# One core, attention and gated feed-forward: P times V of every fourth key tile as three f16 products

## The chip, the core and the metric

The kernel runs on one core of one Trainium2 chip. The metric is the device time of one execution in microseconds (us). Engine names are those of the profile: PE is TensorE's matmuls and PEld its weight loads, DVE is VectorE, ACT is ScalarE, POOL is GpSimd, SP is the queue that issues most DMAs.

## The reference

A block of 2048 rows of width 512, cut to what matters:

```python
h = layernorm(x) * (1 + ca) + sa            # sa, ca, ga, ... = six parts of silu(c) @ w_mod
q = (h @ wq) as 32 heads of 16;  k = h @ wk;  v = h @ wv      # one key and value head for all
p = softmax(q @ k.T * 16 ** -0.5)           # 32 heads x 2048 queries x 2048 keys
x = x + ga * ((p @ v) @ wo)
h = layernorm(x) * (1 + cb) + sb
x = x + gb * (((h @ w_gate) * (h @ w_up)) @ w_down)
```

All inputs are f32. The kernel keeps close to f32 by writing an operand as the sum of two f16 halves and taking three f16 products (high by high, low by high, high by low).

## The kernel before, in words

**Units and turns.** Queries go in 8 blocks of 256 rows, heads in 4 groups of 8. A unit is one group on one block; there are 32 units (0 to 31) of 16 key tiles of 128 keys. `attend(u, kt)` handles key tiles kt and kt+1 of unit u in two turns. In each turn PE computes four score tiles (`qk_exp`, line 648: keys on the rows, 2 heads' parts by 512 columns) and ACT takes the exponential of each (line 661), giving a 128x512 f32 tile of P. At the end of a turn `end_turn` (line 1229) runs `pv` (line 665) for the key tile before: P times V, four f32 matmuls 32 columns wide, one on each quarter of PE's columns, added up in a bank of PSUM over the 16 key tiles. Columns 16 to 31 of V's tile are ones, so the row sums come with it. After the last key tile `pv_out` (line 673) copies the bank out with a factor, `evs`, on ACT (line 676), one turn later.

**The order of a turn** is written out in strings (lines 58 to 60). The one for most of the kernel is

```python
MANY = "x1 e0 x1 m0 x1 e0 x1 e0 x1 m0 x1 m0 x1 m0 x1 e0"
```

An `e` is a score tile with its exponential. An `m` is a matmul for the row maxima of a unit ahead, which DVE reduces (line 605); the maxima enter the scores as two extra rows of the query operand. An `x` is half a step of side work: projections, output projection, gate, up and down (`Group`, line 491; its matmuls are at line 511). Scores and maxima use one half of PE's 128 rows and side work the other, so they run in pairs; the halves are swapped every turn. Since a side bank is then added to from other rows, the first side matmul of a turn waits for the last exponential of the turn before (`sync`, line 527), which follows the last side matmul of that turn.

**Side work around the change.** Each block of 256 rows passes the output projection, the second layer norm, 14 gate and up groups and two down groups. A gate and up group ends with ACT (line 847), DVE (849) and two Pool instructions (850, 851), which write the f16 halves of the gated product to the tile `glu`, double buffered by block. Late weights are staged in slots of the tile `kwb` and split by Pool during units 0 to 8 (`SLOTS`, line 35).

**Order on the engines.** Each engine works in the order in which the program lists its instructions. PSUM has 8 banks, handed out in turn.

The first 66 us hold the layer norm, keys, values, and the row maxima of unit 0.

Of the kernel before, what the change touches and what calls it, by code (L numbers as in the profile page):

```python
# [20 lines left out]
KC = D // 128  # L21
# [13 lines left out]
SLOTS = (0, 1, 2, 3, 6, 7)  # L35
# [6 lines left out]
NBANK = 8  # L42
QPRE = 24
# [20 lines left out]
def adaln_mqa_glu_kernel(ctx: ExitStack, tc: tile.TileContext, x_in, wq_in, wk_in, wv_in, wo_in,  # L64
# [161 lines left out]
    ssqs = [kwb[:, 2 * n * BT:2 * n * BT + 2 * F].bitcast(F32) for n in (KC, 2 * KC)]  # L226
    kng = kwb[:, 2 * NHF * BT:2 * NHF * BT + BT]
# [86 lines left out]
    def v_mm(b):  # L314
        p = ps_hold("pvt", (128, 4, 16))
        for i in range(4):
            nc.tensor.matmul(p[:, i, :], parts[b][:, i * 128:(i + 1) * 128], lane[:, 16:32], start=True, stop=True)

        def out():
            nc.scalar.activation(vst[:, 4 * b:4 * b + 4, 0:16], p, AF.Copy, scale=inv[:, 0:1] if b else 1.0)  # L320
            ps_give(p)
        posts.append(out)
# [48 lines left out]
    kb = consts.tile([128, 8], F32, name="kb")  # L371
    inv = consts.tile([128, 3], F32, name="inv")
# [15 lines left out]
    nc.gpsimd.tensor_scalar(sckb, sck, inv[:, 0:1], 0.0, op0=OP.mult, op1=OP.add)  # L388
    combine(0, selk)
# [9 lines left out]
    evs = consts.tile([128, 1], F32, name="evs")  # L399

    def ev_scales():

        t = work.tile([128, 2], F32, name="evt", bufs=1)
        nc.vector.tensor_reduce(evs, ident.rearrange("p (a r) -> p a r", a=4)[:, :, 0:16], axis=AX.XY, op=OP.add)
        nc.vector.reciprocal(t[:, 0:1], kb[:, 5:6])
        nc.gpsimd.tensor_tensor(t[:, 0:1], t[:, 0:1], evs, op=OP.mult)
        nc.gpsimd.tensor_scalar(t[:, 1:2], evs, -1.0, 1.0, op0=OP.mult, op1=OP.add)
        nc.gpsimd.tensor_tensor(evs, t[:, 0:1], t[:, 1:2], op=OP.add)

# [43 lines left out]
    def last_rows():  # L453
# [21 lines left out]
             15: lambda: h_halves(1, KA), 17: lambda: h_halves(1, KB), 20: ev_scales}  # L475
# [6 lines left out]
    sync = {"due": False, "exp": None, "before": None}  # L482
    pending = []

    def flush():
        for f in pending:
            f()
            sync["due"] = True
        pending.clear()

    class Group:
# [31 lines left out]
        def half(self, r):  # L523

            mm = self.put(r, r + 1)
            if self.rows not in (None, r):
                tc.add_manual_dep(mm.ins, sync["before"], SYNC)
            self.rows, self.turn, sync["due"] = r, now[0], True
            if self.ended():
                ended.append(self)  # L530
# [111 lines left out]
    pvb = {}  # L642
    ptl = {}
    oc = {}
# [3 lines left out]
    def qk_exp(u, kt, p, a, last=False):  # L648
        s = sst[u % 3]
        ptl[u, kt, p, a] = work.tile([128, D], F32, name="P", tag="P", bufs=8)  # L650
        t = ps_sc()
        keys = kst[64 * a:64 * a + 50, kt * 128:(kt + 1) * 128]
        if pending and last:
            for c in range(2):
                if c:
                    flush()
                nc.tensor.matmul(t[:, c * ST:(c + 1) * ST], keys, s[64 * a:64 * a + 50, c, p, :], start=True, stop=True)  # L657
        else:
            nc.tensor.matmul(t.rearrange("k (c n) -> k c n", c=2), keys, s[64 * a:64 * a + 50, :, p, :],  # L659
                             start=True, stop=True)  # L660
        ex = nc.scalar.activation(ptl[u, kt, p, a], t, AF.Exp)  # L661
        if sync["due"]:
            sync.update(due=False, exp=ex.ins.name)

    def pv(u, kt):
        if kt == 0:
            pvb[u] = ps_hold("pv")
        for j in range(4):
            p, a = divmod(j, 2)
            nc.tensor.matmul(pvb[u][32 * j:32 * j + 32, :], vst[:, kt, :], ptl[u, kt, p, a],  # L670
                             start=(kt == 0), stop=(kt == KT - 1))

    def pv_out(u):
        sb, ch = divmod(u, NC)
        ev = work.tile([128, BT], F32, name="ev", tag="ev", bufs=3)
        nc.scalar.activation(ev, pvb[u], AF.Copy, scale=evs)
# [115 lines left out]
    def ln2_work(sb):  # L792
        st = {}

        def tr(i):
            def f():
                if not h2s:
                    h2T = big.tile([128, 2, 2, KC, ST], F16, name="h2T", tag="wq")
                    glus.append(big.tile([128, 2, 2, FT, ST], F16, name="glu", tag="big"))
                    h2s.update({s: h2T[:, s % 2] for s in range(NS)})  # L800
# [31 lines left out]
    def ffn_work(sb):  # L832

        def glu():
            return glus[0][:, sb % 2]
# [57 lines left out]
    def late_weights():  # L893
# [37 lines left out]
        def stage(n):  # L931
            if "d" in W:
                t = work.tile([128, D], F32, name="wsl", tag="xl", bufs=3)
            else:
                t = hfs[:, SLOTS[taken[0] % len(SLOTS)], :]
# [237 lines left out]
    side = deque(wlist)  # L1173
# [44 lines left out]
    def attend(u, kt):  # L1218
# [7 lines left out]
        orders = [[(w[0], int(w[1:] or 0)) for w in s.split()] for s in (style if style is NO_SIDE else (style, style))]  # L1226
        count = {}

        def end_turn(kt):
# [5 lines left out]
            ends.clear()  # L1235
            v = u * KT + kt - 1
# [77 lines left out]
    pv(u, KT - 1)  # L1314
    pv_out(u)
# [61 lines left out]
```

## Time and profile before

| | us |
|---|---|
| median of 3 runs (lowest to highest) | 1665.17 (1664.72 to 1667.52) |
| span of the profiled execution, first to last instruction | 1663.8 |
| that execution's own time around the span | not given apart; the median is 1.4 longer than the span |
| PE busy | 1643.3 |
| DVE busy | 1402.3 |
| ACT busy | 1234.8 |
| POOL busy | 523.5 |

A row of the timeline gives the start from the span's beginning, the length, the engine, the line, the operation, what it writes and reads, and how many like instructions were merged. A row of the groups gives the busy time of all and the mean of one in ns. A row of the table by stretches gives, for each engine, busy us and the number of instructions. An f32 matmul appears as two matmul records, each passing over its columns twice.

### The profile page before, as it was taken

To read this page: it belongs to the slowest core of one execution; us is meant where nothing else is said; L and a number is where in the kernel's file an instruction comes from. 1 tells how busy PE (TensorE), PEld (TensorE's weight loads), DVE (VectorE), ACT (ScalarE), POOL (GpSimd) and SP (SyncE) were. 2 spreads that over 40 slices of the span, in tenths; PEclk is the share of its full clock that TensorE was granted. 3 is DMA by queue.
4 is the path that set the end of the run, shared out by engine and by line. 5 is a ranking of instruction groups with operands and counts; after the bars stand their busy time and mean duration, and the time that the engine had idled before them with its cause. 6 is when DMAs were issued, how large, how long until landed. Compare 5 with 4: busy or idle time off the path is not lost.

```text
span 1663.8 us, 39821 instructions
## 1 busy us (share of the span) xinstructions
PE 1643.3 (99%) x15677; PEld 747.1 (45%) x15677; DVE 1402.3 (84%) x2434; ACT 1234.8 (74%) x2389; POOL 523.5 (31%) x833
## 2 busy tenths in 40 slices
PE   8899999999999999999999999999999999999999
PEld 4333333355533554335543355434545345454776
DVE  7999999998998999899998999999998999980211
ACT  5688888888777877777877787777878777877300
POOL 4857537864841111301112011300113001210322
PEclk9999999999999999999999999999999999999999
DMA  6313313342210001000000000000000000000100
GB/s 237 108 59 100 95 43 120 96 129 80 77 51 24 18 12 32 19 32 20 20 26 23 25 13 24 26 25 26 20 29 15 26 22 20 26 14 21 33 13 14
DMA packets 66024, 75.39 MB, mean 45 GB/s; under 512 B 17702, under 2 KB 46634, under 8 KB 65836
## 3 DMA queue, kind: packets, MB, share of 16 engines
q1 hardware_dynamic: 63724, 72.26, 13.7%
q8 instruction: 123, 2.02, 0.5%
q10 hardware_dynamic: 2112, 0.59, 0.1%
q14 instruction: 65, 0.53, 0.1%
HBM read 55.51 MB, written 17.04 MB: 44 GB/s over the span
## 4 chain that ended last, share of the span: by engine, by line
PE 93%; ACT 2%; DVE 2%; DMA 1%; issue 1%; POOL 0%; SPq 0%; ACTq 0%; DVEq 0%
PE side L511 41%; PE pv L670 30%; PE mx L601 8%; PE sc L659 8%; PE sc L657 3%; ACT P L661 2%; DVE mpart L605 1%; DMA xbig<-in_A_x_dram 1%; PE mx L805 1%; PE mxt L629 0%; ACT hf L813 0%; PE sc L601 0%; DVE bs L248 0%; DMA kwb<-in_B_w_down_dram 0%; DMA wkv<-in_A_wv_dram 0%
## 5 line engine op out<-in xcount | busy, mean ns | idle before, releaser
L605 DVE TENSOR_REDUCE mpart<-mx 128x1 f32<-128x512 f32 x2016 | 1274.1, 684 | 104.0 <-PE mx L601 95.7
L661 ACT ACTIVATE P<-sc 128x512 f32<-128x512 f32 x2048 | 1094.8, 598 | 274.2 <-PE sc L659 226.9
L601 PE MATMUL mx<-kst,sst 48*128 48x512 f16 x2032 | 631.5, 377 | 3.8 <-ACT P L661 1.7
L659 PE MATMUL sc<-sst,kst 50*128 50x512 f16 x1792 | 597.5, 379 | 0.6 <-ACT P L661 0.3
L670 PE MATMUL pv<-P,vst 128*32 128x512 f32 x4096 | 545.3, 605 | 0.7
L511 PE MATMUL side<-h2T,wg 64*128 64x256 f16 (+1 forms) x2396 | 540.8, 271 | 0.1
L511 PE MATMUL side<-h2T,wu 64*128 64x256 f16 (+1 forms) x2396 | 538.7, 270 | 0.0
L511 PEld LDWEIGHTS <-wg 64*128 64x128 f16 (+1 forms) x2396 | 226.0, 94 | 230.5 <-ACT P L661 194.0
L511 PE MATMUL side<-wd,glu 64*128 64x512 f16 (+1 forms) x1172 | 272.8, 378 | 0.2 <-ACT P L661 0.2
L850 POOL TENSOR_SCALAR glu<-gf 128x256 f16<-128x256 f32 x112 | 45.8, 409 | 671.3 <-DVE gf L849 583.9
L511 PEld LDWEIGHTS <-wu 64*128 64x128 f16 (+1 forms) x2396 | 226.4, 94 | 43.0 <-issue 7.8
L601 PEld LDWEIGHTS <-sst 48*128 48x128 f16 x2064 | 189.9, 94 | 34.2 <-issue 17.4
L659 PEld LDWEIGHTS <-kst 50*128 50x128 f16 x1792 | 162.9, 94 | 63.0 <-issue 50.3
L511 PEld LDWEIGHTS <-glu 64*128 64x128 f16 (+1 forms) x1172 | 98.5, 94 | 192.4 <-ACT P L661 85.9
L670 PEld LDWEIGHTS pv<-P,vst 128*32 128x32 f32 x4096 | 80.7, 108 | 160.9 <-issue 150.1
L849 DVE TENSOR_TENSOR gf<-side,g 128x256 f32<-128x256 f32 x112 | 46.7, 418 | 79.8 <-ACT g L847 77.7
L657 PE MATMUL sc<-sst,kst 50*128 50x256 f16 x512 | 96.9, 268 | 0.1
L511 PE MATMUL side<-h,wq 64*128 64x512 f16 (+1 forms) x372 | 95.0, 376 | 0.4 <-ACT P L661 0.4
L847 ACT ACTIVATE g<-side 128x256 f32<-128x256 f32 x112 | 42.3, 379 | 65.6 <-PE side L511 65.3
L511 PE MATMUL side<-wo,och 64*128 64x512 f16 (+1 forms) x360 | 86.3, 377 | 0.0
L851 POOL TENSOR_TENSOR glu<-gf,glu 128x256 f16<-128x256 f32 x112 | 75.3, 673 | 9.3
L706 POOL TENSOR_TENSOR oc<-oc,rr 128x256 f32<-128x256 f32 x31 | 22.7, 731 | 146.6 <-DMA rr<-ri 100.4
(233 smaller groups left out, 865.4 us busy)
## 6 DMA issues: line engine op xcount, KB each, us to landing
pd<-ev SPq DMA_DIRECT2D x32, 256.0 KB
kwb<-in_B_w_gate_dram SPq DMA_DIRECT2D x32, 224.0 KB
kwb<-in_B_w_up_dram SPq DMA_DIRECT2D x32, 224.0 KB
sst<-qd SPq DMA_DIRECT2D x180, 32.0 KB
qd<-q SPq DMA_DIRECT2D x16, 256.0 KB
oc<-pd SPq DMA_DIRECT2D x64, 64.0 KB
rr<-ri SPq DMA_DIRECT2D x64, 64.0 KB
x<-in_A_x_dram SPq DMA_DIRECT2D x14, 256.0 KB
```

The lines of the kernel that those rows point to most:

```text
L511: return nc.tensor.matmul(self.p[:, c * w:(c + 1) * w], left[rows], right[rows], start=start and c == 0, stop=stop and c == len(terms) - 1)
L601: nc.tensor.matmul(m, s[64 * a:64 * a + 48, t // 2, p, t % 2 * 128:(t % 2 + 1) * 128], w[64 * a:64 * a + 48, :], start=(i == 0), stop=(i = ...
L605: nc.vector.tensor_reduce(part, m, axis=AX.X, op=OP.max)
L657: nc.tensor.matmul(t[:, c * ST:(c + 1) * ST], keys, s[64 * a:64 * a + 50, c, p, :], start=True, stop=True)
L659: nc.tensor.matmul(t.rearrange("k (c n) -> k c n", c=2), keys, s[64 * a:64 * a + 50, :, p, :], start=True, stop=True)
L661: ex = nc.scalar.activation(ptl[u, kt, p, a], t, AF.Exp)
L670: nc.tensor.matmul(pvb[u][32 * j:32 * j + 32, :], vst[:, kt, :], ptl[u, kt, p, a], start=(kt == 0), stop=(kt == KT - 1))
L706: eng.tensor_tensor(o, o, st["r"], op=OP.mult)
L847: nc.scalar.activation(g, p[:, 0:ST], AF.Copy, scale=2.0 ** -45)
L849: nc.vector.tensor_tensor(gf, p[:, ST:2 * ST], g, op=OP.mult)
L850: nc.gpsimd.tensor_scalar(glu()[:, 0, f, :], gf, 1.0, 0.0, op0=OP.mult, op1=OP.add)
L851: nc.gpsimd.tensor_tensor(glu()[:, 1, f, :], gf, glu()[:, 0, f, :], op=OP.subtract)
```

## The change

- In units 9 to 31 the key tiles 0, 4, 8 and 12 are split: 92 tiles. Their four P tiles go to one of two sets kept in the tile `glu`, which so far held two blocks of gated products and now holds one. Pool writes each P tile as two f16 halves (`p_halves`, one tile per turn, two instructions). V's halves (`v16`) are made once.
- P times V of a split tile is twelve f16 matmuls with their own weight loads instead of four f32 matmuls. It is put off by four key tiles (`pv_turn`): that of tiles 0, 4 and 8 stands where that of the next split tile stood, at the end of a turn, and that of tile 12 stands behind tile 15's, in the next unit's first turn. The end of the next unit's second turn has no P times V.
- In the turn in which a split tile's last exponential runs, a copy of one number on ACT stands before that exponential. It waits for the turn's last side matmul, and the next turn's first side matmul waits for the copy instead of the exponential.
- 14 times ln 2 is added to the exponent by way of the row maxima, so P is 2^14 times larger: one more DVE instruction per unit. The factor `evs` goes, with its two DVE and three Pool instructions; V is scaled instead by `vsc`, made by a DVE reciprocal and a Pool product in the first 25 us.
- The staged weights use slots 12 and 13 instead of 6 and 7, and the scratch for dynamic DMAs is 256 instead of 4096 bytes.

The diff, cut to its core:

```diff
-SLOTS = (0, 1, 2, 3, 6, 7)
+SLOTS = (0, 1, 2, 3, 12, 13)
+EVERY = 4
+SPLIT_FROM = 5
+P_BIAS = float(14 * np.log(2.0))
...
+    nc.vector.reciprocal(vsc[:, 0:1], kb[:, 5:6])
+    nc.gpsimd.tensor_tensor(vsc[:, 1:2], vsc[:, 0:1], inv[:, 0:1], op=OP.mult)
...
-            sync["due"] = True
+            sync.update(due=True, half=f().ins.name)
...
         nc.vector.tensor_reduce(mms[u], mparts[u], axis=AX.X, op=OP.max)
+        nc.vector.tensor_scalar(mms[u], mms[u], -P_BIAS, None, op0=OP.add)
...
+        if last and sync["early"]:
+            ex = nc.scalar.activation(tok[:, 1:2], tok[:, 0:1], AF.Copy)
+            tc.add_manual_dep(ex.ins, sync["half"], SYNC)
+            sync.update(due=False, exp=ex.ins.name)
         ex = nc.scalar.activation(ptl[u, kt, p, a], t, AF.Exp)
...
+    def p_halves():
+        if todo_p:
+            u, kt, p, a = todo_p.popleft()
+            hi, lo = p_view(split_p[u, kt], 2 * a + p)
+            t = ptl[u, kt, p, a]
+            nc.gpsimd.tensor_scalar(hi, t, 1.0, 0.0, op0=OP.mult, op1=OP.add)
+            nc.gpsimd.tensor_tensor(lo, t, hi, op=OP.subtract)
...
+        for n, (vl, pl) in enumerate(((0, 0), (1, 0), (0, 1))):
+            for j in range(4):
+                p, a = divmod(j, 2)
+                nc.tensor.matmul(pvb[u][32 * j:32 * j + 32, :], v16[:, vl, kt // EVERY, :],
+                                 p_view(split_p[u, kt], 2 * a + p)[pl], start=start and n == 0, stop=stop and n == 2)
+
+    def pv_turn(u, kt):
+        if (u, kt) in split_p:
+            late_p.append((u, kt))
+            if len(late_p) > 1:
+                pv(*late_p.popleft())
+        else:
+            pv(u, kt)
+        if kt == KT - 1:
+            while late_p:
+                pv(*late_p.popleft())
+            ends.append(lambda: pv_out(u))
...
-        nc.scalar.activation(ev, pvb[u], AF.Copy, scale=evs)
+        nc.scalar.activation(ev, pvb[u], AF.Copy)
...
-            return glus[0][:, sb % 2]
+            return glus[0]
...
+        if style is MANY and kt % EVERY == 0 and p_sets and not side_items and (u, kt) > (SPLIT_FROM, 0):
+            split_p[u, kt] = len(split_p) % 2
...
+            p_halves()
             v = u * KT + kt - 1
             if v >= 0:
-                pv(*divmod(v, KT))
-                if v % KT == KT - 1:
-                    ends.append(lambda: pv_out(u - 1))
+                pv_turn(*divmod(v, KT))
...
+            sync["early"] = turn == 1 and (u, kt) in split_p
```

Where instructions stand before and now, at three places. On PE, the end of unit 10's first turn, before (`sc` is a score tile, `side` the side work):

```order
5759 L659 LDWEIGHTS kst
5760 L659 MATMUL sc<-sst_129,kst 128x512
5761 L670 MATMUL pv<-P,vst 32x512 x4
5762 L511 LDWEIGHTS glu
5763 L511 MATMUL side<-wd,glu 128x512
```

and after (`v_341` is `v16`; the rows go on in this way to twelve pairs of load and matmul):

```order
5827 L670 LDWEIGHTS kst
5828 L670 MATMUL sc<-sst_129,kst 128x512
5829 L697 MATMUL pv<-P,vst 32x512 x4
5830 L705 LDWEIGHTS v_341
5831 L705 MATMUL pv<-glu,v_341 32x512
5832 L705 LDWEIGHTS v_341
5833 L705 MATMUL pv<-glu,v_341 32x512
```

Tile 12's twelve matmuls of unit 9 moved here, behind tile 15's four.

On ACT, from the late exponentials of unit 8 to the copy of its bank (`ev`), before:

```order
153 L661 ACTIVATE P<-sc 128x512 x12
154 L847 ACTIVATE g<-side 128x256
155 L661 ACTIVATE P<-sc 128x512 x28
156 L634 ACTIVATE mt_7791<-mxt 16x128
157 L661 ACTIVATE P<-sc 128x512 x16
158 L676 ACTIVATE ev<-pv,evs 128x512
```

and after, where unit 9's first split tile (`glu<-sc`) and the small copy (`tok`) stand:

```order
157 L676 ACTIVATE P<-sc 128x512 x8
158 L676 ACTIVATE glu<-sc 128x512 x2
159 L676 ACTIVATE P<-sc 128x512 x2
160 L676 ACTIVATE glu<-sc 128x512 x2
161 L676 ACTIVATE P<-sc 128x512
162 L673 ACTIVATE tok<-tok 1x1
163 L676 ACTIVATE P<-sc 128x512
164 L723 ACTIVATE ev<-pv 128x512
165 L676 ACTIVATE P<-sc 128x512 x8
```

The copy came in before the turn's last exponential; the bank's copy still stands right behind it, ahead of the next turn's exponentials.

On DVE, in the first 25 us, where the first keys are scaled, before:

```order
32 L386 RECIPROCAL fwd<-inv 128x1
33 L387 TENSOR_SCALAR hsb<-modT_178,fwd 128x8
34 L261 TENSOR_SCALAR xbig<-xbig,st,ry_262 128x512 x2
35 L248 BN_STATS bs<-xbig 128x6 x2
36 L250 BN_AGGR st<-bs 128x2 x2
```

and after:

```order
32 L394 RECIPROCAL fwd<-inv 128x1
33 L395 TENSOR_SCALAR hsb<-modT_178,fwd 128x8
34 L397 RECIPROCAL vsc<-kb 128x1
35 L265 TENSOR_SCALAR xbig<-xbig,st,ry_262 128x512 x2
36 L252 BN_STATS bs<-xbig 128x6 x2
```

A reciprocal of a number that Pool makes (`kb`) came in ahead of the layer norm's work.

More of the change, by code (lines that the diff above doesn't have):

```diff
@@ L398, in adaln_mqa_glu_kernel @@
     ln_norm(1, (None, nc.scalar, None, nc.scalar))
[L399 to L408, printed above, removed]
     qvs = consts.tile([128, 1], F32, name="qvs")
@@ L481, in adaln_mqa_glu_kernel @@
     ended = []
-    sync = {"due": False, "exp": None, "before": None}
+    sync = {"due": False, "exp": None, "before": None, "half": None, "early": False}
     pending = []
@@ L527, in half @@
                 tc.add_manual_dep(mm.ins, sync["before"], SYNC)
-            self.rows, self.turn, sync["due"] = r, now[0], True
+            self.rows, self.turn, sync["due"], sync["half"] = r, now[0], True, mm.ins.name
             if self.ended():
```

60 lines of the change are left out of this document (45 added, 15 removed).

## The prediction

> **What bounds the kernel now.** I read the page first: busy times, then the chain that ended last.
>
> ```profile
> PE 1643.3 (99%) x15677; PEld 747.1 (45%) x15677; DVE 1402.3 (84%) x2434; ACT 1234.8 (74%) x2389; POOL 523.5 (31%) x833
> ...
> PE side L511 41%; PE pv L670 30%; PE mx L601 8%; PE sc L659 8%; PE sc L657 3%; ACT P L661 2%; DVE mpart L605 1%; DMA xbig<-in_A_x_dram 1%; PE mx L805 1%; PE mxt L629 0%; ACT hf L813 0%; PE sc L601 0%; DVE bs L248 0%; DMA kwb<-in_B_w_down_dr
> ```
>
> PE carries the chain, and P times V (L670) is 30% of it. The table by stretches then says how near the others are, early and in the stage that the change is about:
>
> ```profile
> 200.00:300.00 100.00, 99.06 (x815) 31.54 (x809) 96.91 (x173) 81.44 (x158) 60.77 (x88) 1.00 0.26 82
> 1000.00:1300.00 300.00, 299.58 (x3045) 136.91 (x3041) 275.41 (x465) 235.40 (x453) 57.66 (x101) 1.00 0.08 23
> ```
>
> Late, PE is full, DVE at 92%, ACT at 78%, POOL at 19%, clock 1.00. Early DVE is at 97%: there an added DVE instruction costs nearly its length. One per cent off PE's late turns is within reach of the other engines.
>
> Last the timeline of three turn ends, at the boundary from unit 17 to 18:
>
> ```profile
> 900.77 1.06 PE L670 MATMUL pv<-P,vst 128*32 128x512 f32 x8
> 901.77 0.39 PE L511 MATMUL side<-wd,glu 64*128 64x512 f16 x1
> 902.23 2.17 ACT L661 ACTIVATE P<-sc 128x512 f32<-128x512 f32 x4 [0.67 <-PE sc L659]
> 903.29 0.38 PE L511 MATMUL side<-wd,glu 64*128 64x512 f16 x1
> 903.61 0.16 PEld L670 LDWEIGHTS pv<-P,vst 128*32 128x32 f32 x8 [0.43 <-ACT P L661]
> 903.61 1.07 PE L670 MATMUL pv<-P,vst 128*32 128x512 f32 x8
> 904.29 0.68 ACT L676 ACTIVATE ev<-pv,evs 128x512 f32<-128x512 f32 x1
> 904.61 0.39 PE L511 MATMUL side<-wd,glu 64*128 64x512 f16 x1
> 905.12 2.09 ACT L661 ACTIVATE P<-sc 128x512 f32<-128x512 f32 x4
> 906.45 1.06 PE L670 MATMUL pv<-P,vst 128*32 128x512 f32 x8
> 907.44 0.39 PE L511 MATMUL side<-wd,glu 64*128 64x512 f16 x1
> ```
>
> A turn is 2.84 us: 1.84 of pairs (the eighth side matmul starts 1.52 in, so a pair takes 0.217) and 1.00 from P times V's start to the next turn. Call a turn's start T. The four exponentials run from T+0.46 to T+2.63, and the next turn's first matmul, which waits for the last of them, starts 0.21 later. Is that wait or PE the bound? Narrower windows of the timeline answer (the last two rows are of a turn that ACT held up):
>
> ```profile
> 901.23 0.61 PE L670 MATMUL pv<-P,vst 128*32 128x512 f32 x4
> ...
> 903.21 1.18 ACT L661 ACTIVATE P<-sc 128x512 f32<-128x512 f32 x2
> ...
> 903.80 0.60 ACT L661 ACTIVATE P<-sc 128x512 f32<-128x512 f32 x1
> ...
> 1433.59 0.60 ACT L661 ACTIVATE P<-sc 128x512 f32<-128x512 f32 x1
> ...
> 1434.24 0.28 PE L511 MATMUL side<-h2T,wg 64*128 64x256 f16 x1
> ```
>
> The four f32 matmuls run side by side in two rounds, 0.46 apart; the second starts 0.54 before the next turn. That is its 0.43 of columns (two passes of 0.213) and 0.10 for the change of tiling. The sum closes without ACT, and it closes alike in every turn above, so PE's own work sets the turn and the wait is hidden by about 0.15 (0.21 less the 0.05 that the last two rows have from ACT's end to PE). ACT's third and fourth exponentials start at T+1.44 and T+2.03, 0.49 apart when nothing is waited for (four in 2.09, the last 0.60 long).
>
> **P times V in f16, behind a turn (tiles 0, 4, 8: 69 of 92).** No f16 matmul 32 columns wide is in this trace. The nearest rows are f32 ones with half the columns, each two passes of 256, as many steps as one pass of 512:
>
> ```profile
> 19.96 1.08 PE L279 MATMUL part<-kwb,wqs 128*32 128x256 f32 x16
> ...
> L279 PE MATMUL part<-kwb,wqs 128*32 128x256 f32 x64 | 4.1, 384 | 0.0
> ```
>
> Sixteen on four column groups are four rounds: (1.08 - 0.38) / 3 = 0.23 a round, stagger included; a pair of f16 matmuls takes 0.217. I take 0.216 a round, as the stagger is paid once, with 0.235 as the upper bound. Three rounds, 0.02 stagger, 0.02 for the first load and 0.10 for the change of tiling: 0.79 instead of 1.00, a gain of 0.21 (0.15 at the upper bound). 69 x 0.21 = **-14.5**. The lower bound of a round is the columns alone, 0.213, which is nearly my value. The weight loads double in number per round, but the row above has eight loads in the first 0.16 us of an operation whose second round starts 0.46 in: loads run ahead of the matmuls there.
>
> [...]
>
> The copy must be done by then: the last side matmul ends at T+1.90 (903.29 + 0.38), the third exponential frees ACT at about T+1.93, and the copy lasts some 0.17, as other tiny ACT instructions do:
>
> ```profile
> L353 ACT ACTIVATE modT<-misc 128x4 f32<-128x4 f32 x1 | 0.2, 172 | 0.0
> ```
>
> It starts at T+2.01 (0.11 behind the matmul, as exponentials are behind their scores) and frees PE at T+2.24, before P times V's end at T+2.63. Hidden; the last exponential moves from T+2.03 to T+2.16 and ends at T+2.76, still before the next turn's first score.
>
> **Tile 12, behind tile 15's P times V (23 times).** No tiling change more, three rounds: 23 x 0.648 = **+14.9**. So the put-off alone gives back what the shorter products gain.
>
> **The turn that has no P times V (23 times).** The next turn may start at T+2.24, when the copy frees it, not T+2.84: 0.60 gained. But the bank's copy (ev, 0.68) stands right behind the last exponential: it starts at T+2.65 and the next exponential some 0.59 after it, T+3.24, where the turn begun at T+2.24 could have had it at T+2.70. Four exponentials 0.49 apart end at T+5.31, and the turn after starts at T+5.37. Before, two turns took 5.69. The gain is 0.33, not 0.60. In 5 of 23 units a side group's evacuation also stands there, and it falls to about 0.05. 18 x 0.33 + 5 x 0.05 = **-6.2** (bounds: none, and 23 x 0.60 = -13.8).
>
> **Pool's splits.** One P tile costs
>
> ```profile
> L441 POOL TENSOR_TENSOR h<-kwb,h 128x512 f16<-128x512 f32 x12 | 13.9, 1162 | 1.0
> L440 POOL TENSOR_SCALAR h<-kwb 128x512 f16<-128x512 f32 x12 | 7.5, 623 | 0.3
> ```
>
> 1.79 us, 1.95 with two gaps of 0.08: 368 of them are 718 us, 1.95 in every 2.84 us turn on an engine that is 19% busy. It fits, with little room. Tiles 0, 4 and 8 have two turns between the last split's place and its use. Tile 12 has one. What stands ahead of that last split on Pool decides; here a gate and up group ends in that very turn (unit 16, tile 14's P times V at 849.72, tile 15's at 852.56):
>
> ```profile
> 849.72 1.06 PE L670 MATMUL pv<-P,vst 128*32 128x512 f32 x8
> 850.95 0.42 DVE L849 TENSOR_TENSOR gf<-side,g 128x256 f32<-128x256 f32 x1
> 851.45 0.41 POOL L850 TENSOR_SCALAR glu<-gf 128x256 f16<-128x256 f32 x1 [7.70 <-DVE gf L849]
> 851.94 0.67 POOL L851 TENSOR_TENSOR glu<-gf,glu 128x256 f16<-128x256 f32 x1
> 852.56 0.64 PE L670 MATMUL pv<-P,vst 128*32 128x512 f32 x4
> ```
>
> Pool, in order, waits for gf, ends glu at 852.61, the split's high half at 853.3 and its low half at 854.55. PE would start tile 12's products at 853.44 and needs the low half in the third, at 853.9: it stands 0.7. By the order this happens in four units (16, 20, 24, 28), and a lateness of 0.2 in three more (21, 25, 29): **+3.4** (bounds: 0, and 0.8 in each of 23: +18).
>
> Does Pool's load slow DVE? DVE's reductions alone, in the same two stretches:
>
> ```profile
> 200.00:300.00 100.00, 91.16 (x147) 1.00 0.26 82
> 1000.00:1300.00 300.00, 259.69 (x410) 1.00 0.08 23
> ```
>
> 0.620 us each with POOL at 61%, 0.633 with POOL at 19%: no. [...]
>
> **The first 25 us.** The new reciprocal stands ahead of the layer norm's work on DVE and waits for a number that Pool makes (timeline, then two rows by line with their lengths in ns):
>
> ```profile
> 20.88 0.23 DVE L387 TENSOR_SCALAR hsb<-modT,fwd 128x8 f32<-128x8 f32 x1
> 21.02 0.99 DVE L261 TENSOR_SCALAR xbig<-xbig,st,ry 128x512 f32<-128x512 f32 x2
> ...
> 22.15 0.26 POOL L377 TENSOR_SCALAR kb<-kb 128x1 f32<-128x1 f32 x1
> ...
> 23.98 0.74 DVE L304 SCALAR_TENSOR_TENSOR sst<-pk,sck,hi 128x512 f16<-128x512 f32 x1
> ...
> 24.78 0.61 PE L601 MATMUL mx<-kst,sst 48*128 48x512 f16 x4
> ...
> L404 DVE TENSOR_REDUCE evs<-ident x1: 218/218/218, 64.0 to 64.0; 128x1 f32<-128x64 f32 x1
> ...
> L405 DVE RECIPROCAL evt<-kb x1: 155/155/155, 64.1 to 64.1; 128x1 f32<-128x1 f32 x1
> ```
>
> Pool has it at 22.41. DVE, free for L261 at 21.02, now stands until about 22.5 and then does the reciprocal (0.15): L261 and all behind it start 1.6 later. Queued behind are the scaling of keys and queries; sst, done at 24.72, feeds PE's matmul at 24.78, and the transposes stand behind that on PE. No slack: +1.6. The two DVE instructions that go (0.22 and 0.15, at 64 us) give back 0.4: **+1.2**.
>
> **The bias** is a 128x16 DVE instruction per unit, 0.2 us like L387's 0.23. In the DVE-bound stretch
>
> ```profile
> 60.00:300.00 240.00, 1.32 (x6) 1.00 0.28 85
> ```
>
> six units' maxima end (the reduction it follows, L622): at most 6 x 0.2; later DVE's 8% of slack hides it. **+0.8.** The slots, the scratch size and the single block of gated products I put at nothing: the first are staged two steps ahead, and a down group ends on PE before the next block's first gate group starts. If that cover is gone, it shows as Pool waits on DMA or PE.
>
> **The sum.** -14.5 + 14.9 - 6.2 + 3.4 + 1.2 + 0.8 = -0.4. Against the profiled span, 1663.8, that is 1663.4; what lies around the span, 1.4 to the median, stays. Forecast: **1664.8 us**, no change. About 0.2%, 3.3 us, is what a measurement of this kernel can tell from none.
>
> **The rivals.**
> - *Faster: Pool is in time and ACT is not late at the unit's boundary.* For it: ACT idles 0.67 in an ordinary turn, so bits of the 0.27 lost there may be caught up. With Pool in time (-3.4) and half of the lost 23 x 0.27 won (-3.1): 1658. With all of it: 1655.
> - *Slower: Pool becomes the wait of every tile 12.* For it: 1.95 of 2.84 us are booked before any gated product (1.2), and one turn is all the slack. The low half is used 4.2 after tile 14's P times V starts (853.9 less 849.72) and the split takes 1.95, so it decides from the point where the last split starts over 2.2 after that. Against it: the four splits take 7.8 in four turns, 11.4, if nothing stands among them. At 0.5 more in each of 23 units: 1664.8 + 11.5 = 1676; at 0.8 in every unit instead of my 3.4: 1680.
> - *Slower: the f16 rounds don't overlap their loads.* A round is then a matmul of 0.38 and a load of 0.11, 0.49: P times V lasts 1.59, and 69 x 0.59 + 23 x 1.47 = +74.5 stands in place of +0.4: 1739. [...] Against it: the eight loads in 0.16.
> - *The change doesn't do what it says: the early copy frees PE no sooner,* being held up as long as the exponential. Then the turn without P times V starts its successor at T+2.68, two turns take 5.52, the gain is 0.17 instead of 0.33 (23 x 0.17 = 3.9 for 6.2): 1667. The order on ACT, where the copy stands ahead, speaks against it.
>
> **How the numbers follow.** The forecast has 0.36 (its own range 1661.5 to 1668.1), faster 0.33, late Pool 0.24, loads 0.03, the copy 0.04; the copy's case is no change too. So faster 0.33, same 0.40, slower 0.27. The range leaves out the loads (0.03), Pool's upper half (0.12) and the best of the faster case (0.05): 1655 to 1676.
>
> **What would show it.** Right: P times V in f16 0.79 from its start to the next turn; 0.65 added behind tile 15; PE idle about 0.5 before the turn that follows none; that turn's exponentials late by 0.5; PE waiting for Pool about 0.7 in units 16, 20, 24, 28; sst at 25.6 instead of 23.98. Wrong: rounds over 0.235, Pool waits in most units, DVE reductions longer than 0.63, or a startup that isn't later.

## The result, and the profile after

The changed kernel takes 1683.21 us, the median of 4 runs (1679.86 to 1685.24), against 1665.47 us for the kernel before, also 4 runs. The ratio is 1.0102, with a 95% interval of 1.0087 to 1.0117. The forecast was 1664.8 with a range up to 1676: the change costs 18 us where nothing was expected. Times of kernels are medians of their executions; one execution of the kernel of number 7, which took 8859.4 us, is left out.

The profiled execution of after is the one of 1679.86 us, with a span of 1678.1. Its busy times and its chain, from the page:

```profile
PE 1637.1 (98%) x16045; PEld 755.5 (45%) x16045; DVE 1407.2 (84%) x2465; ACT 1227.1 (73%) x2481; POOL 1170.5 (70%) x1570
...
PE 80%; DVE 10%; POOL 4%; ACT 3%; issue 1%; DMA 1%; ACTq 0%; POOLq 0%; SPq 0%; DVEq 0%
```

PE is busy 6.2 us less than before, and yet the kernel is longer: PE works less and stands more. DVE's and Pool's shares of the chain say for whom it stands (of DVE's 10 points, 8 are the reductions of L603 and 1 is the new instruction, L621). The waits by who waits for whom, between 480 and 1560 us (columns: waiter, releaser, us in all, times, the longest), name both:

```profile
PEld mx L860 <- POOL n L816: 7.5, 4, 2.3
PE mx L860 <- POOL n L816: 6.1, 3, 2.1
PE mxt L628 <- DVE mm L621: 3.6, 11, 0.6
PE pv L705 <- POOL glu L686: 0.8, 4, 0.2
```

The same view of before has no wait of PE for L816's predecessor (the normalise of the second layer norm, on Pool, L769 there), and one wait of a weight load for the row maxima (`mm`), of 0.8. Only the last row was a term of the prediction. The first three are two mechanisms that it missed, and the timeline shows each. The first two rows are the same stands, seen once by PE's weight loads and once by its matmuls, so they do not add up.

**The normalise, behind the splits.** Unit 17 in after. L753 to L756 write the attention's output, L816 is the normalise, L860 are PE's transposes of its result, L685 and L686 the splits:

```profile
885.05 1.16 POOL L686 TENSOR_TENSOR glu<-glu 128x512 f16<-128x512 f32 x1
...
886.17 0.72 POOL L753 TENSOR_TENSOR oc<-oc,rr 128x256 f32<-128x256 f32 x1
...
887.47 0.67 POOL L756 TENSOR_TENSOR och<-oc,och 128x256 f16<-128x256 f32 x1
887.82 0.14 PEld L860 LDWEIGHTS mx<-ident,n 128*128 128x128 f32 x1 [0.84 <-PE sc L670]
...
888.13 2.07 POOL L816 TENSOR_SCALAR n<-x,st,ry 128x512 f32<-128x512 f32 x1
890.16 0.62 POOL L685 TENSOR_SCALAR glu<-glu 128x512 f16<-128x512 f32 x1
890.25 0.55 PE L860 MATMUL mx<-ident,n 128*128 128x128 f32 x3 [2.11 <-POOL n L816]
...
893.56 1.70 PE L697 MATMUL pv<-P,vst 128*32 128x512 f32 x8
```

PE reaches the transposes at 887.82; Pool, in order, came to the output work (L753 to L756) only when a split ended at 886.21, and starts the normalise at 888.13. PE stands until 890.25. Before, in the same unit, the two were the other way round:

```profile
880.80 2.07 POOL L769 TENSOR_SCALAR n<-x,st,ry 128x512 f32<-128x512 f32 x1
...
885.51 0.42 PEld L805 LDWEIGHTS mx<-ident,n 128*128 128x128 f32 x4 [0.84 <-issue]
```

There the normalise ended 2.64 us ahead of the transposes. The last row of unit 17 shows a second price: P times V lasted 1.70 us instead of 1.06. The clock says why, in this stretch of 10 us (columns as in the prediction's tables by stretches; the clock is the third number from the end; in the two us from 892 to 894 it is 0.50):

```profile
890.00:900.00 10.00, 9.75 (x70) 3.39 (x72) 6.04 (x12) 6.94 (x16) 9.49 (x12) 0.83 0.01 2
```

A mean of 0.83 in 10 us is 3.4 us at half clock, right behind the stand. Unit 17 lasts 3.9 us longer than before, units 21 and 25 each 2.8; units between them differ by 0.4 at most, but for unit 22 (0.7).

**The bias instruction on DVE.** L621 adds 14 ln 2 to the maxima. By the view of the tile `mm` (durations in ns: shortest, median, longest), and then in the timeline of unit 18:

```profile
L620 DVE TENSOR_REDUCE mm<-mpart x32: 220/220/222, 68.6 to 1511.4; 128x16 f32<-128x64 f32 x32
L621 DVE TENSOR_SCALAR mm<-mm x32: 174/421/1023, 68.8 to 1511.7; 128x16 f32<-128x16 f32 x32
```

```profile
943.38 0.22 DVE L620 TENSOR_REDUCE mm<-mpart 128x16 f32<-128x64 f32 x1
943.62 0.62 POOL L685 TENSOR_SCALAR glu<-glu 128x512 f16<-128x512 f32 x1
943.63 0.63 DVE L621 TENSOR_SCALAR mm<-mm 128x16 f32<-128x16 f32 x1
...
944.17 1.28 DVE L603 TENSOR_REDUCE mpart<-mx 128x1 f32<-128x512 f32 x2
...
944.41 0.27 PE L628 MATMUL mxt<-ident,mm 128*16 128x128 f32 x1 [0.39 <-DVE mm L621]
```

Sixteen numbers a row take 0.17 us when Pool is idle, 0.63 when Pool has just begun an instruction of 0.62: L621 ends when Pool's instruction does. So it is in all of the 19 of its 32 instances that last longer than 0.18 us: each ends 0.03 us behind a Pool instruction that began before it. PE's transpose of the maxima (L628) waits for it, and all of the next turn's matmuls stand behind that transpose. The reduction just ahead (L620) always takes 0.22.

Its plain length costs too. In unit 19 it meets no Pool instruction, and the chain that ended last still runs through it (start, length, what):

```profile
990.03 0.23 DVE mm L620
...
990.29 0.17 DVE mm L621
990.46 1.20 DVE mpart L603 x2
...
991.71 0.28 PE sc L670
```

DVE's queue has no gap over 0.04 from 990.03 to 994.56, so the 0.2 for L621 puts off all behind it, and PE's score tile (L670) waits for one of the reductions behind it. In number 5 below, which has no L621, DVE is not on the chain at this place.

**What came as forecast.** The unit boundary from 17 to 18 in after, for the prices of P times V:

```profile
903.62 1.06 PE L697 MATMUL pv<-P,vst 128*32 128x512 f32 x8
904.62 0.39 PE L509 MATMUL side<-wd,glu 64*128 64x512 f16 x1
...
906.46 1.06 PE L697 MATMUL pv<-P,vst 128*32 128x512 f32 x8
...
907.34 0.83 PE L705 MATMUL pv<-glu,v 128*32 128x512 f16 x12
...
908.10 0.39 PE L509 MATMUL side<-wd,glu 64*128 64x512 f16 x1
...
910.07 0.19 ACT L673 ACTIVATE tok<-tok 1x1 f32<-1x1 f32 x1
...
910.31 0.39 PE L509 MATMUL side<-wd,glu 64*128 64x512 f16 x1 [0.30 <-ACT tok L673]
...
910.64 0.58 ACT L723 ACTIVATE ev<-pv 128x512 f32<-128x512 f32 x1
...
913.32 0.39 PE L509 MATMUL side<-wd,glu 64*128 64x512 f16 x1
...
920.97 0.83 PE L705 MATMUL pv<-glu,v 128*32 128x512 f16 x12
...
921.73 0.39 PE L509 MATMUL side<-wd,glu 64*128 64x512 f16 x1
```

f32: 904.62 - 903.62 = 1.00 to the next turn. f16: 921.73 - 920.97 = 0.76. Both behind one another: 908.10 - 906.46 = 1.64. The two turns after that take 913.32 - 908.10 = 5.22.

### The profile page after: what moved, and what is told of

It reads as the page before. It is cut to its first block, busy times and chain, and to the rows that moved or that the text cites. A ratio compares the mean times of both kernels' runs of the same rounds, so it can differ in the third digit from the quotient of the medians.

```text
span 1678.1 us, 41904 instructions
## 1 busy us (share of the span) xinstructions
PE 1637.1 (98%) x16045; PEld 755.5 (45%) x16045; DVE 1407.2 (84%) x2465; ACT 1227.1 (73%) x2481; POOL 1170.5 (70%) x1570
## 3 DMA queue, kind: packets, MB, share of 16 engines
q1 hardware_dynamic: 63724, 72.26, 13.5%
## 4 chain that ended last, share of the span: by engine, by line
PE 80%; DVE 10%; POOL 4%; ACT 3%; issue 1%; DMA 1%; ACTq 0%; POOLq 0%; SPq 0%; DVEq 0%
PE side L509 36%; PE pv L697 22%; PE mx L599 8%; DVE mpart L603 8%; PE sc L670 7%; PE pv L705 3%; PE sc L668 2%; ACT P L676 1%; ACT glu L676 1%; POOL glu L686 1%; POOL n L816 1%; DVE mm L621 1%; DMA xbig<-in_A_x_dram 1%; PE mx L860 1%; POOL glu L685 1%
## 5 line engine op out<-in xcount | busy, mean ns | idle before, releaser
L603 DVE TENSOR_REDUCE mpart<-mx 128x1 f32<-128x512 f32 x2016 | 1268.7, 682 | 112.4 <-PE mx L599 104.2
L676 ACT ACTIVATE P<-sc 128x512 f32<-128x512 f32 x1680 | 913.3, 601 | 154.1 <-PE sc L670 106.9
L670 PE MATMUL sc<-sst,kst 50*128 50x512 f16 x1792 | 601.3, 379 | 1.9 <-ACT P L676 0.3
L697 PE MATMUL pv<-P,vst 128*32 128x512 f32 x3360 | 448.0, 605 | 0.2
L686 POOL TENSOR_TENSOR glu<-glu 128x512 f16<-128x512 f32 x368 | 426.1, 1158 | 30.8
L676 ACT ACTIVATE glu<-sc 128x512 f32<-128x512 f32 x368 | 199.7, 595 | 132.2 <-PE sc L670 122.2
L685 POOL TENSOR_SCALAR glu<-glu 128x512 f16<-128x512 f32 x368 | 227.2, 617 | 86.6 <-ACT glu L676 53.6
L670 PEld LDWEIGHTS <-kst 50*128 50x128 f16 x1792 | 162.9, 94 | 63.3 <-issue 50.3
L905 POOL TENSOR_SCALAR glu<-gf 128x256 f16<-128x256 f32 x112 | 45.7, 408 | 192.8 <-DVE gf L904 191.0
L697 PEld LDWEIGHTS pv<-P,vst 128*32 128x32 f32 x3360 | 66.3, 108 | 134.8 <-issue 126.5
```

The lines of the kernel that those rows point to most:

```text
L603: nc.vector.tensor_reduce(part, m, axis=AX.X, op=OP.max)
L685: nc.gpsimd.tensor_scalar(hi, t, 1.0, 0.0, op0=OP.mult, op1=OP.add)
L686: nc.gpsimd.tensor_tensor(lo, t, hi, op=OP.subtract)
L905: nc.gpsimd.tensor_scalar(glu()[:, 0, f, :], gf, 1.0, 0.0, op0=OP.mult, op1=OP.add)
```

## The experiments

Four theories stood for the 18 us. A: Pool's queue, the normalise behind the splits. C: the bias instruction, which lasts as long as Pool's. D: the reciprocal of V's scale holds up the startup. B, the rival of all: the put-off order and the f16 matmuls themselves. Where a turn is said to be longer or shorter, the time from its first exponential to the next turn's is compared with that of the same turn of before; it is the median over units 9 to 30, and the turns of a unit are numbered 0 to 15. Unit lengths are taken in the same way, from the profiles.

**1. Normalise on ACT**

```diff
-        on_pool = 2 <= sb < NS - 2
+        on_pool = False
```

> The changed kernel, with the second layer norm's normalise on ACT for every block instead of on Pool for blocks 2 to 5. Theory A (Pool's queue: the normalise stands behind the splits, PE's transposes wait for it, and PE's clock falls behind that stand): the three waits of PE for it (13.6 us in units 17, 21 and 25) go, units 17, 21 and 25 lose 2 to 3 us each of their length, and the time falls by 8 to 13 us from 1683, to about 1672. Theory B (the cost is in the put-off order and the f16 matmuls on PE): 1683, no change, the three units no shorter. Theory C (the bias instruction on DVE lasts as long as Pool's instruction): as A for the three units, turn 14 of each unit as long as in the changed kernel.

1675.55 us (ratio to before 1.0055, 1.0043 to 1.0068): 7.7 less than the changed kernel. The waits of L860 for Pool are gone; unit 17 is 0.5 longer than before instead of 3.9, units 21 and 25 are 1.3 and 1.1 instead of 2.8. L621 is as it was (174/442/1052 ns). A holds, just under the low end of what it expected. B falls as the whole of the loss.

**2. Pool's load alone, on the kernel before**

```diff
+    def p_halves():
+        if owed[0]:
+            owed[0] -= 1
+            t, hi, lo = spare[0]
+            nc.gpsimd.tensor_scalar(hi, t, 1.0, 0.0, op0=OP.mult, op1=OP.add)
+            nc.gpsimd.tensor_tensor(lo, t, hi, op=OP.subtract)
...
+        if style is MANY and kt % 4 == 0 and spare and not side_items and u > 5:
+            owed[0] += 4
```

> The kernel before, with nothing but Pool's load added: in the same turns two Pool instructions on tiles of 128x512 that nobody reads, with f32 P times V in its old order. Theory A: the normalise stands behind these instructions, PE's transposes wait for it in units 17, 21 and 25 as in the changed kernel, and the time rises by 7 to 13 us from 1665.5, to about 1675; no late low half and no bias instruction, so nothing else. Theory B: Pool's load alone costs nothing, 1665.5.

1675.05 us (1.0056, 1.0044 to 1.0068): 9.8 above before. It is the cleanest of the runs: every unit from 9 to 30 has the length that it had before, to 0.03 us, but for three, which are longer by 2.10 (unit 17), 2.00 (21) and 3.28 (25). In the view of the normalise's line:

```profile
L779 POOL TENSOR_SCALAR n<-x,st,ry x8: 2072/2082/2096, 679.4 to 1263.1; 128x512 f32<-128x512 f32 x8
...
who waited for it (us, times):
  PEld mx L819: 6.0, 3
  PE mx L819: 5.5, 3
```

Three waits of about 1.9, three longer units. The third is dearer by 1.2, and there the clock drops again:

```profile
1260.00:1270.00 10.00, 8.21 (x74) 4.32 (x70) 5.98 (x10) 5.53 (x11) 9.56 (x12) 0.83 0.01 2
```

So the load, without any f16 matmul, without the new order and without L621, costs what A says, where A says.

**3. Everything but Pool's splits.** The order stays as in the change; split tiles take four f32 matmuls.

```diff
-            hi, lo = p_view(split_p[u, kt], 2 * a + p)
-            t = ptl[u, kt, p, a]
-            nc.gpsimd.tensor_scalar(hi, t, 1.0, 0.0, op0=OP.mult, op1=OP.add)
-            nc.gpsimd.tensor_tensor(lo, t, hi, op=OP.subtract)
...
+        for j in range(4):
+            p, a = divmod(j, 2)
+            nc.tensor.matmul(pvb[u][32 * j:32 * j + 32, :], vst[:, kt, :], ptl[u, kt, p, a], start=start, stop=stop)
```

> The changed kernel without Pool's splits: tiles 0, 4, 8 and 12 are put off as in the change, but their P times V is four f32 matmuls. The f16 gain of some 0.23 us in each of 69 turns is given up (+16) and tile 12's products behind tile 15's cost 1.0 instead of 0.65 (+8). Theory A with C: Pool is as idle as before, so the waits for the normalise go (-8 to -13), the bias instruction lasts 0.17 us (-8 to -11), and there is no late low half (-3); 1683 + 24 - 22 = about 1684, with no wait of PE for Pool in units 17, 21 and 25. Theory B (the order and the matmuls themselves): the losses in units 17, 21 and 25 and in turn 14 stay, 1683 + 24 = about 1705.

1680.09 us (1.0086, 1.0074 to 1.0098), not 1705. The gain of the f16 products is given up, and still the time is no worse: by this run and the expectation's 24, Pool's work costs 1683.2 + 24 - 1680.1 = 27 us in the changed kernel. The 24 is an estimate; turn by turn against number 5, what is given up is 0.92 a unit, 21 in 23 units, which makes it 24. L621 is short again wherever Pool is idle:

```profile
L621 DVE TENSOR_SCALAR mm<-mm x32: 174/175/1029, 69.1 to 1512.3; 128x16 f32<-128x16 f32 x32
```

Its long instances are left where Pool splits weights early on, and in units 17, 21, 25 and 29 beside Pool's splits of the normalised rows (`h2T`), 0.81 to 0.83 there. No unit from 9 on is longer than before by more than 0.81, and PE waits for Pool's normalise nowhere.

**4. The bias in the exponential**

```diff
+    nc.gpsimd.memset(pbias, P_BIAS)
...
-        nc.vector.tensor_scalar(mms[u], mms[u], -P_BIAS, None, op0=OP.add)
...
-        ex = nc.scalar.activation(ptl[u, kt, p, a], t, AF.Exp)
+        ex = nc.scalar.activation(ptl[u, kt, p, a], t, AF.Exp, bias=pbias[:, 0:1])
```

> The changed kernel, with the 14 ln 2 as the bias of ACT's exponential instead of as an instruction of DVE on the row maxima. Theory C (that instruction lasts until Pool's running one ends, and PE's transposes of the maxima wait for it): the fourteenth turn of a unit loses 0.4 to 0.6 us in units 9 to 31, some 2 us of the shift before unit 8 goes, and the time falls by 8 to 13 us from 1683, to about 1673. Theory A alone: 1683, since Pool's queue is as it was; so does theory B. If PE's transposes then wait for the reduction itself as long, the instruction was only a bystander: 1683.

1727.16 us (1.0377, 1.036 to 1.0393): a miss, and no test of C, because the edit has a price of its own that the expectation left out. The exponentials, by line:

```profile
L677 ACT ACTIVATE P<-sc,pbias 128x512 f32<-128x512 f32 x1680 | 1036.6, 688 | 90.6 <-PE sc L671 70.4 <-PE mx L601 10.7 <-PE side L511 1.9
```

688 ns instead of the 601 of after: the bias operand costs each of 2048 exponentials 0.09 us, and ACT's four per turn become the bound: ACT has 21% of the chain, in after 3%.

**5. The bias where it is free.** PE turns the maxima with an identity that holds 1/32, and the two instructions that read the result add the number in place of their factor.

```diff
+    nc.scalar.activation(ident32, ident, AF.Copy, scale=1.0 / 32.0)
...
-        nc.vector.tensor_scalar(mms[u], mms[u], -P_BIAS, None, op0=OP.add)
...
-            nc.tensor.transpose(p, mms[u].rearrange("p a c -> p (a c)"), ident)
+            nc.tensor.matmul(p, mms[u].rearrange("p a c -> p (a c)"), ident32, start=True, stop=True)
...
-            nc.scalar.activation(mt[0], p, AF.Copy, scale=1.0 / 32.0)
-            nc.vector.scalar_tensor_tensor(mt[1], p, 1.0 / 32.0, mt[0], op0=OP.mult, op1=OP.subtract)
+            nc.scalar.activation(mt[0], p, AF.Copy, bias=-P_BIAS / 32.0)
+            nc.vector.scalar_tensor_tensor(mt[1], p, -P_BIAS / 32.0, mt[0], op0=OP.add, op1=OP.subtract)
```

> The changed kernel, with the 14 ln 2 added where it costs no instruction: PE turns the maxima with an identity that holds 1/32, and ACT's and DVE's two instructions that read the result from PSUM, whose factor 1/32 is thus free, add the number instead. The exponentials have no operand for a bias, so they last 0.60 us again, not 0.69 as in the run with the bias in the exponential. Theory C (the instruction on the maxima lasts until Pool's running one ends, and PE stands for it): 0.35 to 0.45 us less in turn 14 of units 9 to 31, 2 to 4 us less before unit 9, so 1683 - 12 = about 1671, between 1669 and 1675. Theory that PE would stand there anyway (for the reduction ahead of it): 1683.

1669.75 us (1.0025, 1.0015 to 1.0034): 13.5 less than the changed kernel. Turns 13 and 14 together fall from +0.26 to -0.20, so 0.46 at the median. Over the 22 units that have the instruction (9 to 30) it is 9.3 in all; 2.5 lie ahead of unit 9 in the two profiles, and the other 1.7 are within what executions differ by. The two instructions that read the result last 266 and 272 ns with the number, in after 265 and 269 with the factor. No wait of PE for a DVE instruction on `mm` is left in units 9 to 31. C holds, but it is not all of it: in units 11, 15, 19, 23 and 27, where L621 had its plain 0.17, turns 13 and 14 are shorter by 0.20 to 0.21 all the same; where it lasted 0.6 to 0.7 they are mostly shorter by 0.6 to 0.7, and where about 1.0, by 0.8 to 1.0. So the plain length is an estimated 22 x 0.2 = 4.4 of the 9.3, and Pool's lengthening the other half. The waits for the normalise are all still there:

```profile
PE mx L861 <- POOL n L817: 6.2, 3, 2.1
```

**6. The reciprocal later**

```diff
-    nc.vector.reciprocal(vsc[:, 0:1], kb[:, 5:6])
-    nc.gpsimd.tensor_tensor(vsc[:, 1:2], vsc[:, 0:1], inv[:, 0:1], op=OP.mult)
     combine(0, selk)
...
     ln_norm(1, (None, nc.scalar, None, nc.scalar))
+    nc.vector.reciprocal(vsc[:, 0:1], kb[:, 5:6])
+    nc.gpsimd.tensor_tensor(vsc[:, 1:2], vsc[:, 0:1], inv[:, 0:1], op=OP.mult)
```

> The changed kernel, with the reciprocal and the product that make V's scale listed behind the layer norm's last part instead of ahead of it. Theory D (the reciprocal's wait for Pool holds up DVE's queue, and with it the scaled queries and PE's first score matmuls): the first exponential comes 1.0 to 1.3 us earlier, and the time falls by as much from 1683, to about 1682. Rival (the startup's slack is elsewhere): the first exponential is not earlier, 1683.

1683.16 us (1.0103, 1.0089 to 1.0116): no change. The scaled queries (`sst`) did come earlier, at 23.61 us, where after has 24.76 and before 23.98, but the first exponential came at 77.39, after's at 77.23. Between the two lies a stretch whose clock differs from execution to execution, here and then in after:

```profile
40.00:50.00 10.00, 8.63 (x53) 5.59 (x55) 8.88 (x15) 8.52 (x20) 6.35 (x9) 0.83 0.66 274
```

```profile
40.00:50.00 10.00, 8.36 (x60) 4.78 (x56) 10.00 (x17) 9.51 (x20) 7.42 (x10) 1.00 0.75 306
```

The last two kernels below have one and the same startup, and their first exponentials are at 76.66 (clock 0.83 there) and 75.70 (1.00). So the clock alone is worth a microsecond, and this run against after leaves D open. Kernels with the same clock in that stretch settle it: at 0.83, numbers 1 and 7 with the early reciprocal have 78.48 and 78.35, this one 77.39; at 1.00, numbers 4 and 5 with the early one have 76.76 and 76.51, numbers 8 and 11 with the late one 75.69 and 75.70. That is 0.8 to 1.1 in each pair. D holds, though the medians, whose runs differ by more, do not show it.

**7. Without the small copy**

```diff
-            sync["early"] = turn == 1 and (u, kt) in split_p
+            sync["early"] = False
```

> The changed kernel without the small copy: the first side matmul of the next turn waits for the last exponential, as in the kernel before. If the copy does what the prediction says: an f16 P times V ends 0.1 before the last exponential would free PE, so 69 turns lose 0.05 to 0.1 each (3 to 7), and the second turn of a unit, which has no P times V, loses 0.2 to 0.4 (5 to 9): 1691 to 1699. If the copy frees PE no sooner than the exponential: 1683.

1689.59 us (1.0142, 1.0126 to 1.0157): 6.4 more, so the copy works, a little below the least that was expected. Turns 1 and 2 of a unit together are 0.36 longer than with it, turns 5 and 9, each with an f16 P times V, 0.06 to 0.07; turn 13, where DVE holds PE up, is no longer than with it.

**8. Three edits together, with the bias in the exponential, and 9. the same with tile 12 carried over.** The first has the edits of 1, 4 and 6. The second also puts tile 12's products where the next unit has no P times V:

```diff
         if (u, kt) in split_p:
             late_p.append((u, kt))
             if len(late_p) > 1:
-                pv(*late_p.popleft())
+                pv_last(*late_p.popleft())
         else:
-            pv(u, kt)
-        if kt == KT - 1:
-            while late_p:
-                pv(*late_p.popleft())
+            pv_last(u, kt)
+
+    def pv_last(u, kt):
+        pv(u, kt)
+        if did_pv[u] == KT:
             ends.append(lambda: pv_out(u))
...
+    while late_p:
+        pv_last(*late_p.popleft())
```

> The changed kernel with three edits at once: normalise on ACT, bias in the exponential, reciprocal later. Theories A, C and D together, and adding up: 1683 - 10 - 10 - 1 = 1662, between 1659 and 1666, so a little faster than the kernel before or the same. If the stalls hide one another (turns are held by ACT or by Pool's late halves instead): 1668 to 1675. Theory B: 1683.

> As the kernel with the three edits, and tile 12's products are no longer put behind tile 15's in the next unit's first turn but at the end of its second turn, which has no P times V. If the boundary's cost is the 0.65 of these twelve matmuls against the 0.4 that the turn without P times V gains: the boundary gains some 0.4 us in each of 23 units, and the late low halves (0.58 in four units, 0.25 in two) go: 10 to 13 us below the kernel with the three edits, about 1650, and 15 below the kernel before. If ACT's lag behind the bank's copy sets the boundary: 1660.

1725.42 us (1.0355, 1.0341 to 1.0369) and 1707.36 us (1.0246, 1.0232 to 1.026). Both missed for the reason of number 4: ACT is the bound. Between the two, carrying over is worth 18 us.

**10 and 11. The same two with the free bias**

> Normalise on ACT, V's reciprocal later, and the bias added to the transposed maxima: theories A, C and D add up, 1683 - 7.5 - 12 - 1 = about 1662.5, between 1660 and 1666. If the losses hide one another: 1668 to 1675. What is left against the plain sum of the prediction (-14.5 + 14.9 - 6.2 + late halves 3.4) is then what the change gives without its side effects.

> As the last one, and tile 12's products stand at the end of the next unit's second turn, which had no P times V, instead of behind tile 15's in its first. With the bias in the exponential this took 18 us off (1725.4 to 1707.4), with ACT as the bound. With PE as the bound it should give 23 x 0.4 for the boundary and some 3 for the late low halves: 1662.5 - 12 = about 1650, between 1646 and 1655, below the kernel before. If ACT's lag sets the boundary: 1658 to 1662.

1659.69 us (0.9969, 0.9957 to 0.9981) and 1648.13 us (0.9898, 0.9885 to 0.9912). The first is 0.3 below the low end of what was expected, the second within it: the losses add up, and without them the change is a gain of 0.3%. Carried over, it is a gain of 1.0%, the fastest of all the kernels here. Both are measured against the kernel before as it is; the kernel before with its normalise on ACT was not run, so what that edit alone would do there is not shown. The chain of this last kernel:

```profile
PE 92%; ACT 3%; DVE 2%; DMA 1%; issue 1%; POOL 1%; ACTq 0%; SPq 0%; DVEq 0%; POOLq 0%
```

PE has 12 points more of the chain than in after, and DVE and Pool have 11 fewer. Its first two turns of a unit are 0.06 longer and 0.36 shorter than before, where those of number 10 are 0.71 longer and 0.39 shorter.

## Why the prediction was wrong

Against its own terms, in its order:

- **P times V in f16 behind a turn, -14.5.** Right, a little better: 0.76 instead of 0.79 from its start to the next turn, against 1.00 before: 69 x 0.234 = -16.1. The rounds take 0.216, as assumed, and their loads are hidden, so that rival fell: twelve matmuls in 0.83.
- **Tile 12 behind tile 15's, +14.9.** Right: 1.64 for both where one takes 1.00.
- **The turn without P times V, -6.2.** The mechanism right, the gain larger. The copy frees PE at T+2.21 (forecast 2.24; T is 908.10), and then the bank's copy `ev` starts at T+2.54 instead of T+2.65 and lasts 0.58 instead of 0.68, as it no longer has its factor as an operand. Two turns take 5.22 instead of 5.37. PE stood 0.27 for the copy on average (23 times, 6.3 us), where the prediction's sign was about 0.5. Over the units, the first three turns are longer by 0.71 - 0.39 - 0.13 = 0.19 in all, so that 0.46 of tile 12's 0.65 comes back: 23 x 0.46 = -10.6.
- **Late low halves, +3.4.** Right in what stood ahead of them and nearly in size; of the seven places, unit 29 had none. Unit 16's boundary in after:

```profile
853.20 0.41 POOL L905 TENSOR_SCALAR glu<-gf 128x256 f16<-128x256 f32 x1 [1.94 <-DVE gf L904]
...
853.69 0.67 POOL L906 TENSOR_TENSOR glu<-gf,glu 128x256 f16<-128x256 f32 x1
...
854.32 0.62 POOL L685 TENSOR_SCALAR glu<-glu 128x512 f16<-128x512 f32 x1
854.32 1.07 PE L697 MATMUL pv<-P,vst 128*32 128x512 f32 x8
...
855.03 1.16 POOL L686 TENSOR_TENSOR glu<-glu 128x512 f16<-128x512 f32 x1
...
856.24 0.38 PE L705 MATMUL pv<-glu,v 128*32 128x512 f16 x1 [0.21 <-POOL glu L686]
856.55 0.39 PE L509 MATMUL side<-wo,och 64*128 64x512 f16 x1
```

  From 854.32 to 856.55 are 2.23 instead of 1.64. It is 0.58 in units 16, 20, 24 and 28 and 0.25 in 21 and 25: +2.8. Not foreseen was the last unit, where no turn covers tile 12's splits: from the P times V of tiles 14 and 15 to the bank's copy it takes 4.20 (1561.96 to 1566.16) where before took 2.34. Of these 1.9 more, 0.65 are tile 12's own products and in the +14.9 already: +1.2.
- **The startup, +1.2.** About +0.4. DVE stood 0.8 for the reciprocal's number, not 1.6, and its place costs 0.8 to 1.1 (number 6). What was taken away gives back about 0.5: with the late reciprocal and without L621 the first exponential is at 75.69 and 75.70, in before at 76.18, all at clock 1.00.
- **The bias, +0.8: the first step that failed.** The runs put it at 13.5. It was priced as a short DVE instruction hidden by "DVE's 8% of slack". That slack is a mean over 300 us; from the instruction to the end of turn 14 DVE has none (unit 19 above), so its plain 0.2 was not hidden: about 4.4 (number 5). And it lies on the way from the maxima to PE's transpose, which PE reaches in order, and it lasts until Pool's instruction ends, up to 1023 ns instead of 174: the other half of what it costs in units 9 to 30. The prediction's question "does Pool's load slow DVE?" was answered for the reductions alone, and for them the answer stands: 682 ns on average in after, 684 before. The one DVE instruction that the change adds to every unit is of another kind. The trace of before had a row of that kind, the layer norm's scaling on DVE, an f32 TENSOR_SCALAR of the same shape on both lines (shortest, median and longest, in ns):

```profile
L261 DVE TENSOR_SCALAR xbig<-xbig,st,ry x6: 537/544/847, 11.2 to 31.4; 128x512 f32<-128x512 f32 x6
L261 DVE TENSOR_SCALAR P<-P,st,ry x2: 833/1102/1371, 41.6 to 42.4; 128x512 f32<-128x512 f32 x2
```

  The second line's stand among Pool's splits of weights. That spread, up to 2.5 times the shortest, was the price to ask about. In after L621 lasted 174 to 1023 ns, by what Pool had running, while the reduction ahead of it (L620) kept its 220 to 222. Why Pool holds up the one kind and not the other, no run shows.
- **Pool's splits, +3.4 in all: the second step that failed.** The term counted only the splits' own lateness. Bounded "0.8 in each of 23", it asked who waits for the splits and not who stands behind them on Pool's queue. The normalise does, and in unit 17 its 2.64 us of lead became 2.4 of lateness; units 21 and 25 went the same way. Priced by the edit that removes it: 7.7, some of it the half clock behind PE's stand. The prediction had the rule in its own check of the gated products' two instructions ahead of a split, and did not turn it round.
- **The slots, the scratch and the single block, 0.** No loss shows: Pool's waits on DMA between 66 and 480 us are 8.1 in after and 10.1 in before, no write of a gated product (L905) waits for PE from 480 us on, and units 0 to 8 of number 10 are 2.4 shorter than in before, for a reason that no run shows.

The sum with what was measured: -16.1 + 14.9 - 10.6 + 2.8 + 1.2 + 0.4 + 13.5 + 7.7 = +13.8, against 17.7 by the medians and 14.3 by the two profiled spans. What is left is of the size by which the runs of after differ among themselves (5.4).

Of the rivals, "Pool becomes the wait of every tile 12" named the right engine and the wrong work: tile 12 waited in six boundaries, where the forecast had seven. Its 1676 lies nearer to the result than the forecast, for a reason that it did not give.

Not settled: when the half clock follows such a stand. Six kernels have three stands each: after and numbers 2, 4, 5, 6 and 7. It began within 1.7 us of a stand's end in unit 17 of after, 25 of number 2, 21 and 25 of number 5, 17 and 25 of number 6, 17 and 21 of number 7, and behind none of the other ten. From 480 to 1560 us none came in the profiles of before and of numbers 1, 3 and 8 to 11, which have no such stand.

## What to carry to other kernels

When a queue in order gets new work, list who stands behind it and who waits for them, not only who waits for the new work. Before calling a small instruction hidden, look at whether an engine that is never idle waits for its result, at the slack of its own engine in the very turn where it stands (a mean over hundreds of turns hides a full one), and at rows of its own kind beside the load that the change adds: here rows of another kind on the same engine (reductions of 682 ns on average with Pool's splits, 684 without) told nothing of an instruction that went from 174 to as much as 1023. When a change comes out even or worse, undo its side effects one at a time: here a gain of 1% was under a loss of 1%.

## What the runs showed of the hardware

- A DVE TENSOR_SCALAR of 128x16 from SBUF to SBUF (L621 in after) took 174 to 176 ns in 13 of 32 instances, where Pool was idle or done within its first 0.12 us. In the other 19 it took 397 to 1023 beside Pool instructions of 0.56 to 1.16 us, behind whose end it ended by 0.03 us each time. A TENSOR_REDUCE to the same tile took 220 to 222 in all cases.
- A bias operand made ACT's exponential of 128x512 last 688 ns (number 4) instead of 601 (after); the bank's copy went from 688 (before) to 595 (after) when it lost its scale operand.
- PE had 3.4 us at half clock (a mean of 0.83 in 10 us, and in after 0.50 inside them) behind eight of eighteen stands of 1.6 to 2.1 us.
